# Weight loads of 448 rows over all 128 partitions, paired x loads, attention input copies on GpSimd, and a new issue order

## The chip, the core and the metric

The kernel runs on one core of a Trainium2 chip. The metric is device time in microseconds (us), from one launch to its end; the time before is the median of three runs. The core has a matrix engine (TensorE, in the profile PE for matmuls and PEld for weight loads), a vector engine (DVE), a scalar engine (ACT), GpSimd (POOL), and SyncE (SP), which here only issues DMAs. ACT issues a few DMAs too. The rows "SPq" and "ACTq" are these issues.

## What is computed

One block of a network on 2048 tokens of 448 features, in bf16: local dilated attention with 16 heads of 28 features, then a gated MLP that mixes over tokens with a 2048 by 2048 matrix.

```python
def _A_ref(x, wqkv, wo):                       # x: 1 x 2048 x 448
    qkv = (x @ wqkv).reshape(B, S, 3, 16, 28)  # q, k, v
    idx = pos[:, None] - 2 * arange(8)         # 8 keys, every second token back
    attn = softmax(q . k[idx] * 28 ** -0.5)    # masked where idx < 0
    return (attn . v[idx]).reshape(B, S, D) @ wo
def _B_ref(x, w_in, w_sp, b_sp, w_out):
    z = gelu(x @ w_in)                         # 1792 features
    z1, z2 = z[..., :896], layernorm(z[..., 896:])
    g = w_sp @ z2 + b_sp[None, :, None]        # mixes over the 2048 tokens
    return (z1 * g) @ w_out
h  = x + _A_ref(layernorm(x), wqkv, wo)
h2 = h + _B_ref(layernorm(h), w_in, w_sp, b_sp, w_out)
```

## The kernel before, in words

**Tiling.** The 2048 tokens are two halves of 1024. The normalised and transposed activations lie in `xh`, with features on partitions: the first half's tokens on partitions 0 to 63, the second half's on 64 to 127, and the 448 features as seven blocks of 64 rows along the free axis. A matmul has 64 rows, and two of them, one for each half, run side by side on the upper and the lower rows of the array. Each weight matrix therefore lies twice in SBUF: on partitions 0 to 63 and again on 64 to 127, block c on both at free index c.

**Loads.** `ld_w` (L542) loads each of Wq, Wk and Wv with two DMAs of 392 KB, the lower copy from SP and the upper copy from ACT, each to 64 partitions. Wq and Wk are staged in `z2p` and copied (L729, `cp`) into padded form in `reg1`; Wv goes straight to `reg1`. `ld_win` (L552) loads the MLP's input weights with eight DMAs of 64 partitions, `ld_x` (L536) the tokens with sixteen DMAs of 112 KB, and L920 loads Wo four times over 28 partitions each. In the profile, `z2p<-in_A_wqkv` is Wq or Wk, `reg<-in_A_wqkv` is Wv, `reg<-in_A_wo` is Wo.

**Stages.** For each unit u of 128 tokens of both halves: layer norm 1 (`bn_stats` L617, `bn_aggr` L622, the reciprocal root on ACT L633/634 or POOL L608/609, the normalisation L641 into `tring`), and the transpose into `xh`, for units 0 to 2 by PE (L657) with a copy out of PSUM, for units 3 to 7 by a transposing DMA (L648). Then the q and k matmuls (L759) and, for each of nine attention tiles i, a copy `xv` of 128 columns of `xh` (L797), v (L807), logits (L838), exp (L852), mask (L860), row sums (L873), log and exp of the reciprocal (L882, L907), the weighted sum (L896) and its scaling (L915). After that, unit by unit, Wo (L951), the residual (L960), layer norm 2, the MLP's z2 (L972) and z1 (L1015), and finally the token mixing g (L1049), its bias and gate (L1059, L1066), the output matmul (L1075), the last sum (L1083) and the store.

**Order.** The tuple SEQ holds a task order for each engine (sp, pool, dve, act, pe in this order), by task number. `replay` walks these lists and emits the instructions; engines run them strictly in that order and wait on semaphores. The numbers in `replay` (`bw`, `issue`, `costs`) choose PSUM banks and buffers and otherwise move nothing.

## Time and profile before

| | us |
|---|---|
| median of 3 runs | 258.79 (258.0 to 260.02) |
| the profiled execution: its time | 258.7 |
| the profiled execution: its span | 257.0 |
| PE busy | 233.9 (91%) |
| DVE busy | 135.6 (53%) |
| ACT busy | 89.8 (35%) |
| POOL busy | 26.0 (10%) |

A span is the time from the first to the last instruction in the trace; 1.7 us of the run's time lie outside it. Busy shares are averages over very different stages: PE is busy nearly throughout, so what counts is where it is not, and what it waits for there.

### The profile page before, as it was taken

The numbers are of one execution on the slowest core, as the hardware profiler recorded it, in microseconds if no ns is written. First come the engines' busy times: TensorE is split into PE (matmuls) and PEld (weight loads), VectorE is DVE, ScalarE is ACT, GpSimd is POOL, SyncE is SP. The second block draws the span as 40 slices with busy tenths as digits, with TensorE's granted clock in tenths as the row PEclk, the third lists the DMA queues.
The fourth block names the chain that finished last, engine by engine and source line by source line (L and its number), as shares of the span: only waits on it lengthen the run. The fifth ranks groups of instructions, "written<-read, shape, count | busy, mean of one in ns | idle before, by whom it ended". The sixth has DMA issues, their size and how long they took to land.

```text
span 257.0 us, 6304 instructions
## 1 busy us (share of the span) xinstructions
PE 233.9 (91%) x2822; PEld 123.2 (48%) x2822; DVE 135.6 (53%) x286; ACT 89.8 (35%) x107; POOL 26.0 (10%) x67
## 2 busy tenths in 40 slices
PE   0298987998688999999999999999999999999995
PEld 0276754456344585554444444444444444444542
DVE  4378946737477996977773015210063127442444
ACT  3369876599448664556574000000000000000000
POOL 7202400000100213202180000000000000000000
PEclk9999999999779999999999999999999999999999
DMA  6995089648959378898454634200000000001013
GB/s 172 207 249 106 13 121 191 77 109 146 179 70 190 70 106 210 158 151 115 95 130 77 167 81 86 44 0 0 0 3 0 0 0 3 18 0 54 26 64 126
DMA packets 57235, 23.22 MB, mean 90 GB/s; under 512 B 46696, under 2 KB 57080, under 8 KB 57208
## 3 DMA queue, kind: packets, MB, share of 16 engines
q1 hardware_dynamic: 55528, 21.38, 44.1%
q10 hardware_dynamic: 1680, 1.43, 2.4%
q8 instruction: 22, 0.36, 0.6%
q14 instruction: 5, 0.04, 0.1%
HBM read 9.60 MB, written 1.84 MB: 44 GB/s over the span
## 4 chain that ended last, share of the span: by engine, by line
PE 75%; DVE 9%; DMA 7%; ACT 4%; issue 2%; SPq 2%; POOL 1%
PE psum L1049 38%; PE psum L1075 8%; PE psum L1015 6%; PE psum L951 5%; PE psum L972 5%; DMA x_tm<-in_A_x_dram 5%; PE psum L759 5%; PE psum L807 3%; DVE tring L641 2%; DVE st L617 2%; DMA xh<-tring 2%; PE psum L896 2%; PE psum L838 1%; DVE st L988 1%; DVE xv L605 1%
## 5 line engine op out<-in xcount | busy, mean ns | idle before, releaser
L1059 DVE TENSOR_TENSOR reg<-psum,reg 128x512 bf16<-128x512 f32 x28 | 18.8, 688 | 70.8 <-PE psum L1049 60.1
L1049 PE MATMUL psum<-reg,z2p 128*128 128x512 bf16 x224 | 50.1, 379 | 0.0
L1049 PE MATMUL psum<-wspT_lo,z2p 128*128 128x512 bf16 x224 | 49.5, 379 | 0.0
L1049 PEld LDWEIGHTS psum<-wspT_lo,z2p 128*128 128x128 bf16 x224 | 21.8, 98 | 26.6 <-DVE z2p L1002 0.4
L1049 PEld LDWEIGHTS psum<-reg,z2p 128*128 128x128 bf16 x224 | 21.9, 98 | 26.1
L759 PE MATMUL psum<-xh,reg 64*128 64x256 bf16 (+2 forms) x336 | 27.3, 317 | 1.8 <-ACT reg L603 1.6
L603 ACT ACTIVATE reg<-psum 128x1024 bf16<-128x1024 f32 (+2 forms) x24 | 21.3, 920 | 10.5 <-PE psum L807 5.3
L972 PE MATMUL psum<-w_in,xh 64*128 64x448 bf16 x224 | 22.5, 349 | 0.3 <-DMA xh<-tring 0.3
L1075 PE MATMUL psum<-reg 128*128 128x448 bf16 x112 | 22.2, 352 | 0.0
L1015 PE MATMUL psum<-xh,w_in 64*128 64x512 bf16 x196 | 21.7, 376 | 0.0
L759 PEld LDWEIGHTS psum<-xh,reg 64*128 64x128 bf16 x336 | 16.6, 98 | 10.4 <-ACT reg L907 2.0
L617 DVE BATCH_NORM_STATS2 st<-x_tm 128x6 f32<-128x448 bf16 x32 | 18.8, 614 | 4.6 <-DMA x_tm<-in_A_x_dram 4.6
L988 DVE BATCH_NORM_STATS2 st<-z2p 128x6 f32<-128x448 bf16 x32 | 17.6, 610 | 3.8 <-ACT z2p L982 3.8
L807 PE MATMUL psum<-reg,xv 64*128 64x448 bf16 x126 | 15.1, 378 | 4.0 <-ACT reg L852 2.7
L982 ACT ACTIVATE z2p<-psum 128x896 bf16<-128x896 f32 x16 | 14.1, 918 | 9.8 <-PE psum L972 9.8
L852 ACT ACTIVATE reg<-psum 128x928 bf16<-128x928 f32 x18 | 16.3, 950 | 2.7 <-PE psum L838 2.6
L972 PEld LDWEIGHTS psum<-w_in,xh 64*128 64x128 bf16 x224 | 12.8, 94 | 9.1 <-DMA xh<-tring 1.1
L1025 ACT ACTIVATE reg<-psum 128x1024 bf16<-128x1024 f32 x14 | 13.7, 1026 | 8.1 <-PE psum L1015 8.1
L1075 PEld LDWEIGHTS psum<-reg 128*128 128x128 bf16 x112 | 11.0, 98 | 10.6
L915 DVE TENSOR_TENSOR reg<-psum,reg 128x912 bf16<-128x912 f32 x9 | 10.8, 1225 | 9.6 <-ACT reg L907 8.2
L1015 PEld LDWEIGHTS psum<-xh,w_in 64*128 64x128 bf16 x196 | 10.3, 94 | 10.7 <-issue 0.2
L951 PE MATMUL psum<-reg 64*128 64x448 bf16 x128 | 15.0, 377 | 0.2 <-ACT reg L603 0.2
(63 smaller groups left out, 183.8 us busy)
## 6 DMA issues: line engine op xcount, KB each, us to landing
w_in<-in_B_w_in_dram SPq DMA_DIRECT2D x4, 448.0 KB, 6.3
out_dram<-tring SPq DMA_DIRECT2D x16, 112.0 KB, 1.7
x_tm<-in_A_x_dram SPq DMA_DIRECT2D x14, 112.0 KB, 9.9
w_in<-in_B_w_in_dram SPq DMA_DIRECT2D x4, 336.0 KB, 4.9
z2p<-in_A_wqkv_dram ACTq DMA_DIRECT2D x2, 392.0 KB, 6.8
z2p<-in_A_wqkv_dram SPq DMA_DIRECT2D x2, 392.0 KB, 9.6
reg<-in_A_wo_dram SPq DMA_DIRECT2D x4, 196.0 KB
reg<-in_B_w_out_dram SPq DMA_DIRECT2D x1, 784.0 KB, 4.8
```

The source lines that it names most:

```text
L603: iss("act", lambda e: e.activation(dst, src, AF.Copy), reads=rd, writes=wr)
L617: iss("dve", lambda e: e.bn_stats(st[:, b, :], x_tm[:, b, :]), reads=[r_x[b]], writes=[rl[b]])
L759: iss("pe", lambda e, c=c, s=s, gi=gi, lhs=lhs: e.matmul(psum[:, bk[s] * 512 + cw * gi:bk[s] * 512 + cw * gi + cw], lhs, xh[64 * s:64 * s ...
L807: iss("pe", lambda e, c=c, s=s: e.matmul(psum[:, bk[s] * 512:bk[s] * 512 + D], xv[64 * s:64 * s + 64, xs[0], c, :], wv[64 * s:64 * s + 64, ...
L852: iss("act", lambda e: e.activation(E[:, es[0], 2 * n:2 * n + 2, :], pair_view(lb, 8 * JW), AF.Exp, scale=SCALE), reads=[r_bank[lb[0]], r_ ...
L951: iss("pe", lambda e, s=s, x=x: e.matmul(psum[:, bk[s] * 512:bk[s] * 512 + D], oT[64 * s:64 * s + 64, x, 128 * u:128 * u + 128], wo2[64 * ...
L972: iss("pe", lambda e, c=c, s=s: e.matmul(psum[:, zb[s] * 512:zb[s] * 512 + D], xh[64 * s:64 * s + 64, c, HX + 128 * u:HX + 128 * u + 128], ...
L988: iss("dve", lambda e, b=b: e.bn_stats(st3[:, b, k, :], z2p[:, b, D * k:D * k + D]), reads=[r_z2[b][k]], writes=[r_st3[b][k]])
L1015: iss("pe", lambda e, c=c, s=s: e.matmul(psum[:, bk[s] * 512:bk[s] * 512 + 512], w_in[64 * s:64 * s + 64, c, 128 * f:128 * f + 128], xh[64 ...
L1049: iss("pe", lambda e, b=b: e.matmul(psum[:, gb[0] * 512:gb[0] * 512 + 512], z2p[:, b, 128 * f:128 * f + 128], src[:, b, 512 * (tc % 2):512 ...
L1059: iss("dve", lambda e: e.tensor_tensor(ub[:, us_[0], :], psum[:, gb[0] * 512:gb[0] * 512 + 512], bb[:, 512 * tc:512 * tc + 512], ALU.add), ...
L1075: iss("pe", lambda e, f=f: e.matmul(psum[:, wb[0] * 512:wb[0] * 512 + D], z1p[f][:, 128 * m:128 * m + 128], w_out[:, f, :], start=(f == 0) ...
```

## The change

Each 448-row weight is now loaded by `ld_rows`: rows 0 to 383 as three blocks of 128 rows over all 128 partitions, rows 64 to 447 in the same way, and two pieces of 64 rows for the seventh index. The bytes are the same (896 rows). The row blocks then stand in another order on the upper than on the lower partitions; `ROWS` holds that order, and the matmuls take the block of `xh` that it names. This holds for Wq, Wk, Wv (four DMAs each, two from SP and two from ACT) and for both halves of w_in (four each from SP). Tokens come in four single blocks and six pairs. Wo is loaded once (two DMAs), and a copy of 64 x 3584 makes the second one (`cpwo`, which the new lists put on POOL). The `xv` copies may also go to POOL, and the new lists put all nine there. All five lists of SEQ are new.

```diff
-XV_ON = ("dve", "act")
+XV_ON = ("dve", "act", "pool")
+ROWS = ((0, 2, 4, 1, 3, 5, 6), (1, 3, 5, 2, 4, 6, 0))
 SEQ = (
-    (0, 4, 6, 19, 2, 13, 12, 7, 17, 21, 14, 20, 11, 16, 22, 9, 277, 18, 69, 15, 97, 76, 83, 90, 284, 276, 288, 279, 289,
+    (8, 0, 6, 2, 4, 11, 9, 18, 17, 22, 19, 15, 20, 13, 21, 69, 83, 280, 97, 76, 90, 287, 277, 288, 279, 285, 276, 289,
...
-        def ld_x(b, eng="sp"):
-            t_x[b] = dma(eng, "x%d" % b, lambda e: e.dma_start(x_tm[:, b, :], X[128 * b:128 * b + 128, :]),
-                         128 * D * 2, writes=[r_x[b]])
+        def ld_x(bs, eng="sp"):
+            b0, n = bs[0], len(bs)
+            t = dma(eng, "x%d" % b0, lambda e: e.dma_start(
+                x_tm[:, b0:b0 + n, :], X[128 * b0:128 * (b0 + n), :].rearrange("(b p) n -> p b n", p=128)),
+                128 * D * 2 * n, writes=[r_x[b] for b in bs])
...
+        def ld_rows(name, dst, src, res, engs, issue):
+            w = src.shape[1] * 2
+            parts = ((dst[:, 0:3, :], src[0:384, :].rearrange("(k p) n -> p k n", p=128), 384, 0),
+                     (dst[:, 3:6, :], src[64:448, :].rearrange("(k p) n -> p k n", p=128), 384, 1),
+                     (dst[0:64, 6, :], src[384:448, :], 64, 2),
+                     (dst[64:128, 6, :], src[0:64, :], 64, 3))
+            return [dma(engs[n % len(engs)], "%s%d" % (name, n), lambda e, d=d, f=f: e.dma_start(d, f), rows * w,
+                        writes=[res[k]], issue=issue if rows > 64 else 0.42) for n, (d, f, rows, k) in enumerate(parts)]
...
-            t_w[p] = [dma(eng, "w%s%d" % (p, s), lambda e, s=s: e.dma_start(
-                w_ld[p][64 * s:64 * s + 64], A_wqkv[:, c0:c0 + D].rearrange("(c p) n -> p c n", p=64)),
-                D * D * 2, writes=[r_ld[p][s]], issue=0.65, bw=350.0) for s, eng in ((0, "sp"), (1, "act"))]
+            t_w[p] = ld_rows("w" + p, w_ld[p], A_wqkv[:, c0:c0 + D], r_ld[p], ("sp", "act"), 0.6)
...
+            t_win[z] = ld_rows("win%d_" % z, w_in[:, :, FH * z:FH * z + FH], B_w_in[:, FH * z:FH * z + FH], r_win[z], ("sp",), 0.6)
...
-                                        xh[64 * s:64 * s + 64, c, off + t0:off + t0 + cw],
+                                        xh[64 * s:64 * s + 64, ROWS[s][k], off + t0:off + t0 + cw],
...
-        for n in range(4):
-            s, e_ = n // 2, n % 2
-            t_wo.append(dma("sp", "wo%d" % n, lambda e, s=s, e_=e_: e.dma_start(
-                wo2[64 * s + 32 * e_:64 * s + 32 * e_ + DH, :, :],
-                A_wo.rearrange("(g h d) n -> h d g n", g=8, h=2)[e_]), DH * 8 * D * 2,
-                writes=[r_wo[n]], deps=[c_wo0], bw=100.0))
+        for e_ in range(2):
+            t_wo.append(dma("sp", "wo%d" % e_, lambda e, e_=e_: e.dma_start(
+                wo2[32 * e_:32 * e_ + DH, :, :], A_wo.rearrange("(g h d) n -> h d g n", g=8, h=2)[e_]), DH * 8 * D * 2,
+                writes=[r_wo[e_]], deps=[c_wo0], bw=160.0))
+        tk = []
+        tk.append(add("cpwo", "pool", 3.6, lambda: copy(tk[0].eng, wo2[64:128], wo2[0:64], r_wo[0:2], [r_wo[2]]), deps=t_wo,
+                      alts={"pool": 3.6, "dve": 1.10, "act": 3.15}))
```

Where the new lists move work, at three places. First SP at the start of the program. Before (`x_tm` is the tokens, 16x448 a halo of the first half's last tokens):

```order
L537 DMA x_tm<-in_A_x_dram 128x448 x2
L567 DMA z2p<-in_A_x_dram 16x448
L537 DMA x_tm<-in_A_x_dram 128x448
L544 DMA z2p<-in_A_wqkv_dram 64x7x448
L537 DMA x_tm<-in_A_x_dram 128x448 x2
L544 DMA z2p<-in_A_wqkv_dram 64x7x448
L537 DMA x_tm<-in_A_x_dram 128x448 x7
L544 DMA reg<-in_A_wqkv_dram 64x7x448
L922 DMA reg<-in_A_wo_dram 28x8x448
L537 DMA x_tm<-in_A_x_dram 128x448
```

SP at the same place after the change:

```order
L572 DMA z2p<-in_A_x_dram 16x448
L539 DMA x_tm<-in_A_x_dram 128x448
L551 DMA z2p<-in_A_wqkv_dram 64x448
L539 DMA x_tm<-in_A_x_dram 128x448
L551 DMA z2p<-in_A_wqkv_dram 128x3x448
L551 DMA z2p<-in_A_wqkv_dram 64x448
L551 DMA z2p<-in_A_wqkv_dram 128x3x448
L539 DMA x_tm<-in_A_x_dram 128x2x448 x4
L551 DMA reg<-in_A_wqkv_dram 64x448
L539 DMA x_tm<-in_A_x_dram 128x2x448
L551 DMA reg<-in_A_wqkv_dram 128x3x448
L539 DMA x_tm<-in_A_x_dram 128x2x448
```

SP's share of Wq and Wk now stands directly behind the two token blocks that the first unit pair needs, with no other token block between them, and a Wo load is gone from this place. ACT issues its own two token blocks and then the other pieces of Wq and Wk.

Second, DVE between the last loads of tokens and the first row sums. Before:

```order
L605 COPY xh<-psum 128x7x128
L617 BN_STATS st<-x_tm 128x6
L622 BN_AGGR mv<-st 128x2 x2
L617 BN_STATS st<-x_tm 128x6
L622 BN_AGGR mv<-st 128x2 x4
L641 TENSOR_SCALAR tring<-x_tm,mv,rs 128x2x7x32 x2
L605 COPY xv<-xh 128x896
L641 TENSOR_SCALAR tring<-x_tm,mv,rs 128x2x7x32
L605 COPY xv<-xh 128x896
L641 TENSOR_SCALAR tring<-x_tm,mv,rs 128x2x7x32
L860 TENSOR_TENSOR reg<-reg,mband 128x928 x2
L641 TENSOR_SCALAR tring<-x_tm,mv,rs 128x2x7x32 x4
```

DVE at the same place after the change:

```order
L610 COPY xh<-psum 128x7x128
L622 BN_STATS st<-x_tm 128x6
L646 TENSOR_SCALAR tring<-x_tm,mv,rs 128x2x7x32 x2
L622 BN_STATS st<-x_tm 128x6 x3
L627 BN_AGGR mv<-st 128x2 x2
L865 TENSOR_TENSOR reg<-reg,mband 128x928
L627 BN_AGGR mv<-st 128x2 x2
L646 TENSOR_SCALAR tring<-x_tm,mv,rs 128x2x7x32
L865 TENSOR_TENSOR reg<-reg,mband 128x928
L627 BN_AGGR mv<-st 128x2 x2
L646 TENSOR_SCALAR tring<-x_tm,mv,rs 128x2x7x32 x3
```

The `xv` copies are gone from DVE, and the first masks (L865, before L860) stand earlier among the normalisations.

Third, POOL after the change, from the first `xv` copy to the first layer norm 2. Before, POOL has only the rs pairs, the mask's and the ones' set-up in this place:

```order
L610 COPY xv<-xh 128x896
L613 TENSOR_SCALAR rs<-mv 128x2
L614 TENSOR_TENSOR rs<-rs,nhalf 128x2
L610 COPY xv<-xh 128x896
L597 MEMSET reg 64x1792
L610 COPY xv<-xh 128x896
...
L710 MEMSET ones 128x32
...
L610 COPY xv<-xh 128x896 x2
L610 COPY reg<-reg 64x3584
L610 COPY xv<-xh 128x896
L613 TENSOR_SCALAR rs<-mv 128x2
```

The row `COPY reg<-reg 64x3584` is `cpwo`. The Wo matmul (L951 before, L958 after) reads its result. On PE that matmul stood behind 96 logit matmuls, and now its first unit stands ahead of them; before:

```order
L759 MATMUL psum<-xh,reg 128x512 x28
L807 MATMUL psum<-reg,xv 128x448 x14
L838 MATMUL psum<-reg 64x58 x96
L951 MATMUL psum<-reg 128x448 x32
L896 MATMUL psum<-reg 32x58 x32
```

PE at the same place after the change:

```order
L878 MATMUL psum<-reg,ones 32x464 x8
L901 MATMUL psum<-reg 32x58 x32
L764 MATMUL psum<-xh,reg 128x512 x28
L958 MATMUL psum<-reg 128x448 x16
L843 MATMUL psum<-reg 64x58 x96
```

The v matmuls that stood between the last q and k matmuls and these logits now come earlier.

## Rows read from the trace of the kernel before

**Rows 1.** Stages: busy (instructions) by PE, PEld, DVE, ACT, POOL; clock, DMA, GB/s

```profile
0.00:10.00 10.00, 1.67 (x14) 1.41 (x14) 4.36 (x14) 3.10 (x6) 6.00 (x22) 1.00 0.85 188
20.00:30.00 10.00, 9.27 (x245) 6.59 (x241) 8.78 (x27) 9.36 (x16) 4.45 (x13) 1.00 0.27 57
...
10.00:12.00 2.00, 0.00 (x0) 0.00 (x0) 0.24 (x1) 0.25 (x1) 0.00 (x0) 1.00 1.15 198
16.00:18.00 2.00, 2.00 (x40) 1.75 (x38) 2.00 (x4) 0.57 (x2) 0.00 (x0) 1.00 1.13 282
112.00:254.00 142.00, 141.68 (x792) 65.64 (x786) 55.83 (x124) 17.30 (x19) 7.93 (x16) 1.00 0.25 52
```

**Rows 2.** The chain that ended last, its end: start, length, what

```profile
136.14 76.08 PE psum L1049 x352
...
254.17 0.62 DVE tring L1083
```

**Rows 3.** Timeline of the start: start, length, instruction, idle before it

```profile
11.76 0.62 DVE L605 COPY reg<-z2p 128x1568 bf16<-128x1568 bf16 x1 [4.09 <-DMA z2p<-in_A_wqkv_dram]
12.30 0.48 DVE L682 TENSOR_SCALAR z2p<-z2p,mvh,rsh 16x448 bf16<-16x448 bf16 x1
12.71 0.60 DVE L605 COPY xh<-psum 128x896 bf16<-128x896 bf16 x1
13.36 7.55 PE L759 MATMUL psum<-xh,reg 64*128 64x256 bf16 x112 [0.18 <-DVE xh L605]
21.07 1.50 PE L807 MATMUL psum<-reg,xv 64*128 64x448 bf16 x14 [0.15 <-DMA reg<-in_A_wqkv_dram]
23.51 1.54 PE L838 MATMUL psum<-reg 28*64 28x58 bf16 x128
```

**Rows 4.** The chain between 27 and 40 us

```profile
27.99 0.99 DVE xv L605
...
35.08 0.44 PE psum L873 x8
```

**Rows 5.** Timeline of PE: stalls between 34 and 90 us, and the first Wo matmul

```profile
35.08 0.39 PE L873 MATMUL psum<-reg,ones 64*32 64x464 bf16 x8 [0.51 <-DVE reg L605]
39.86 3.20 PE L759 MATMUL psum<-xh,reg 64*128 64x512 bf16 x28 [1.55 <-ACT reg L603]
58.77 3.20 PE L951 MATMUL psum<-reg 64*128 64x448 bf16 x32 [0.17 <-ACT reg L603]
66.29 1.96 PE L807 MATMUL psum<-reg,xv 64*128 64x448 bf16 x14 [2.68 <-ACT reg L852]
73.53 0.21 PE L896 MATMUL psum<-reg 64*32 64x58 bf16 x6 [1.28 <-issue]
83.69 2.63 PE L807 MATMUL psum<-reg,xv 64*128 64x448 bf16 x25 [1.17 <-issue]
```

**Rows 6.** Instructions on tile xv: ns least/median/most, first and last start

```profile
L605 DVE COPY xv<-xh x7: 1069/1079/1085, 16.4 to 79.9; 128x896 bf16<-128x896 bf16 x7
L603 ACT ACTIVATE xv<-xh x2: 960/972/984, 13.3 to 61.0; 128x896 bf16<-128x896 bf16 x2
```

**Rows 7.** Timeline of POOL: its longest instruction

```profile
2.10 1.59 POOL L592 MEMSET reg<- 128x1792 f32 x1
```

**Rows 8.** Stages of 2 us after the stall at 66 us

```profile
66.00:68.00 2.00, 1.71 (x14) 0.92 (x15) 1.05 (x3) 0.07 (x1) 0.78 (x2) 0.80 1.12 241
68.00:70.00 2.00, 2.00 (x14) 1.03 (x12) 0.00 (x0) 0.92 (x1) 0.15 (x1) 0.50 1.08 207
70.00:72.00 2.00, 2.00 (x99) 1.08 (x95) 0.97 (x1) 0.62 (x1) 0.00 (x0) 0.85 0.92 150
```

**Rows 9.** Timeline of SP: the second token-mix transpose and the fourth Wo load

```profile
46.20 1.17 SPq L932 DMA_TRANSPOSE wspT_lo<-in_B_w_sp_dram  x1
47.41 0.56 SPq L922 DMA_DIRECT2D reg<-in_A_wo_dram  x1
```

**Rows 10.** Tile reg (Wv, Wo and later loads): DMA issue to landing

```profile
DMA to landing us min/median/max: 4.0/5.3/11.4
```

86 lines of the change are left out of this document (41 added, 45 removed), and 57 rows, old and new, of the table SEQ.

## The prediction

> **What bounds the kernel now.** I read the stages first, then the chain that ended last, then the timelines of the two places that they point to.
>
> From 112 us to 254 us PE is busy 141.68 us of 142 [rows 1], and the chain of that stretch is matmuls alone, up to the last sum on DVE at 254.17 and the last store [rows 2]. The change keeps every matmul there, so that half stays as long as it is, and so does the tail behind it. What can move is when PE gets there: its idle time and slow stretches before 90 us.
>
> There are three kinds. *The start.* In the first 10 us PE is busy 1.67 us [rows 1]. Its first q and k matmul runs at 13.36, directly behind three DVE instructions: the copy of Wq (11.76, which had waited 4.09 us for the load), the halo's normalisation (12.30) and the copy of unit 1 into `xh` (12.71) [rows 3]. Those three run without a gap, so Wq's landing sets PE's start. *The middle.* Between 20 and 30 us PE is busy 9.27, ACT 9.36 and DVE 8.78 us of 10 [rows 1], all three near their limit; the chain there runs through DVE, with `xv` copies on it, to the row sums at 35.08 [rows 4]. PE waits 0.51 us for DVE at 35.08, 1.55 at 39.86 and 2.68 at 66.29 for ACT [rows 5]. *Stalls in which the engine waited for nothing that the profile shows*: 1.28 us at 73.53 and 1.17 at 83.69 [rows 5]. After the stall at 66.29 the granted clock is 0.80, 0.50 and 0.85 in three stages of 2 us, which is the level of 1.2 instead of 2.4 GHz for part of them [rows 8]; the loss is 2 x (0.20 + 0.50 + 0.15) = 1.7 us.
>
> **The change, part by part.**
>
> *Weights over 128 partitions, and their place in the queue.* Wq and Wk lie behind 14 KB of halo and four token blocks of 112 KB on both queues together: 14 + 448 + 2 x 784 = 2030 KB, or 2.08 MB, and nothing else. The first 10 us moved 188 GB/s on average, issue and first latency included [rows 1]; at that pace 2.08 MB are there at 11.05 us. That is the bound without any faster transfer. Between 10 and 12 us, when the old 64-partition weight loads filled the queue, the rate was 198 GB/s; between 16 and 18, with token blocks over 128 partitions among them, 282 [rows 1]. If all 1.6 MB of Wq and Wk went at 282 in place of 198, they would take 1.6 x (1/198 - 1/282) x 1000 = 2.4 us less, so 8.6 us at best. I take 10.2, nearer to the slow end, because both weights now finish together, with Wq's last piece behind Wk's large one on ACT. The halo's normalisation now stands ahead of the copy on DVE, so PE starts at 10.2 + 0.62 + 0.60 and about 0.1 of gaps = 11.5, against 13.36: **1.9 us earlier**, with bounds of 1.0 and 3.4.
>
> The Trainium skill ("SBUF — State Buffer", Door 1: The DMA port swizzle) says that a transfer to one half of the partitions reaches only half of the DMA ports, and that only one transfer over all 128 reaches all of them. The stage rows lean its way, 198 against 282 GB/s, though they mix kinds of transfers; if it holds fully the start is at its 3.4 us bound.
>
> This gain must survive Wv, which PE met at 21.07 with a wait of 0.15 us [rows 3]. Its last pieces stand behind all but two token blocks, and ACT issues its share only after its copies of Wq and Wk. The same faster rate over 2.35 MB of weights gives Wv up to 3.5 us; I need 1.9. If the rate stays, PE waits there and the gain is 0.5 us, because PE now does unit 2's transposes while it waits.
>
> *More, smaller DMAs.* There are six more issues of weights and six fewer of tokens. ACT issues three more, at about 0.6 us each; they lie between its Wq and Wk copies, and the k matmuls follow 56 q matmuls that hide them. Nothing is added.
>
> *w_in.* Eight loads before and after, needed only at about 90 us; hidden behind the whole attention, and the mixing of row blocks costs the matmuls nothing, since their shapes are the same.
>
> *xv copies to POOL.* DVE loses seven copies of 1.08 us and ACT two of 0.97 [rows 6]. The DVE ones between 16 and 42 us lie on or next to the chain. POOL has no such copy in this trace. Its longest instruction writes 1792 elements per partition in 1.59 us, or 0.89 ns per element [rows 7], so 896 elements take 0.8 us if reading is free and 1.6 us if reading costs as much as writing. I take 1.1, nearest the same work on DVE and ACT. Queued behind them on POOL are the rs pairs of later units, which can slip by one copy, and behind these the normalisations; that hands back a part of what DVE gains.
>
> What this is worth is bounded by PE's waits: 0.51 + 1.55 us at 35 and 40 us, and 2.68 us at 66 [rows 5], so 0 to 4.74. The first two hang on masks and row sums that come about three copies late on DVE, so I take both, 2.06. The third is ACT's own queue of exps and logarithms, which loses one copy and one eviction; I take 0.3. **2.4 us earlier.**
>
> *Wo once, and a copy.* This adds a link. The second load of Wo now stands behind the second token-mix transpose and two w_in loads, where before the fourth load followed that transpose (46.20, 47.41) [rows 9]: about 48.6 with 1.2 us more of issues, less what SP gains from the two terms above, so near 45. Landing takes 5.3 us in the median of such loads [rows 10], then POOL copies 3584 elements: 3.2 us by its rate of writing, 6.4 at twice that. The end is 53.5 to 56.7, or later if `xv` copies stand ahead. PE wants Wo at 58.77 now [rows 5], and then 4.3 us earlier and 1.0 us more because 96 logit matmuls have moved behind it: 53.4. So PE waits 0.1 to 3.3 us; a part of that only replaces the wait at 66.29. **0.6 us later.**
>
> Sum: -1.9 - 2.4 + 0.6 = -3.7 us. The profiled execution took 258.7 us, 1.7 of them outside its span of 257.0; it lies at the median, so the forecast is 253.3 of span and **255.0 us** of time.
>
> **The rivals.**
>
> *The Wo copy decides (slower).* If POOL copies at 6.4 us or more and two `xv` copies of 1.6 us stand ahead, Wo is ready at 60. PE then waits 6.6 us at its first Wo matmul, and the clock drops after it as it did after the stall at 66.29, another 1.7: -4.3 + 6.6 + 1.7 = +4.0, so 262.8. For: everything on PE queues behind that matmul. Against: POOL is busy only 10% of the span before, so little stands ahead of the copy. It decides from a copy that ends after about 57.7, where the gain is gone; beyond 58.6 with the clock's drop the kernel is slower by over 1%.
>
> *POOL holds up DVE (no change).* Nine `xv` copies and a Wo copy four times as long are 13 copies; at 0.8 us that is 10.4 us. If DVE stood still for all of it, it would lose 10.4 and gain 7.6, so the middle's 2.4 us are gone and about 1 more: -1.9 + 0.6 + 1.0 = -0.3, or 258.4. For: DVE is busy 8.78 us of 10 in that stage [rows 1], so the two must overlap. Against: no row of this trace has either engine held up by the other. The Trainium skill (same page, Who interferes with whom) speaks for it: GpSimd and some DVE instructions share a pair of ports, and the later one blocks fully. By that the case would be likelier; this trace cannot tell.
>
> *The gain is spent in ACT's queue (no change).* Both waits that I count most end on ACT. If PE merely comes earlier to the same ACT queue, only the start counts: 258.7 - 1.9 + 0.6 = 257.4.
>
> *More falls away.* The two stalls without a visible cause (2.45 us) and the drop of the clock (1.7 us) may not come again in another order: 255.0 - 4.1 = 250.9. For: they follow heavy transfers, 241 and 207 GB/s at 66 to 70 us [rows 8]. Against: others can come in their place.
>
> **How the numbers follow.** A measurement of this kernel tells a difference of about 1% (2.6 us) from none. The forecast, 251.5 to 256.2, has 0.46; more falls away, 0.15; the two cases without change together 0.25; slower by the Wo copy or by a stall like it 0.14. The likeliest is the forecast. The range leaves out the far part of the last case (0.1) and little below the best (0.1): 250.0 to 260.5. Faster by over 1%: 0.46 + 0.15 = 0.61; within 1%: 0.25; slower: 0.14.
>
> **What would show it.** In the new profile the first q and k matmul stands near 11.5; the Wq copy on DVE starts near 10.2, and the rate between 4 and 10 us is above 220 GB/s. DVE has no `xv` row, and POOL's are near 1.1 us. PE has no wait over 1 us between 30 and 45 us. The first Wo matmul stands near 54 with a wait under 2 us. From 110 us to the end PE's length is the same to half a microsecond. I am wrong if Wq still lands after 11.5, if PE waits on POOL before its first Wo matmul by more than 3 us, or if a new stall before 90 us brings a second drop of the clock.

## The result and the profile after

| | before | after |
|---|---|---|
| median of the runs, us | 258.79 [258.0 to 260.02] | 252.05 [249.79 to 254.25], four runs |
| ratio to the kernel before, same chip | | 0.964, 95% interval 0.952 to 0.975 |
| the profiled execution: time, us | 258.7 | 250.46 |
| the profiled execution: span, us | 257.0 | 248.7 |
| PE busy, us | 233.9 | 231.4 |
| POOL busy, us | 26.0 | 40.7 |

The kernel became faster, and by more than the forecast of 3.7 us: by 6.7 us between the two medians, by 9.4 after the ratio, and by 5.6 in a second set of runs on another chip (median 252.95, ratio 0.978, 0.974 to 0.983). The ratio of 0.964 compares the two fast runs among the four, 249.8 and 250.5 us and not 253.6 and 254.3, with a median of 259.4 us of four runs of the kernel before. What parts its two groups of times is not shown; the experiments have two candidates.

The first view is one of three stretches of each kernel: up to the first q and k matmul, from there to the first Wo matmul, and from there to the first matmul of the token mix (136.08 us before, 127.75 after). Columns as in [rows 1].

```profile
0.00:13.36 13.36, 2.03 (x21) 1.68 (x22) 5.96 (x18) 4.63 (x8) 6.00 (x22) 1.00 0.92 190
13.36:58.77 45.41, 41.93 (x1053) 26.76 (x1054) 29.98 (x59) 34.91 (x45) 4.45 (x13) 1.00 0.67 125
58.77:136.08 77.31, 71.86 (x1189) 40.05 (x1189) 60.84 (x135) 48.52 (x55) 15.58 (x32) 0.96 0.76 132
```

The same three stretches of the changed kernel:

```profile
0.00:10.57 10.57, 1.96 (x21) 1.67 (x21) 6.36 (x17) 4.43 (x7) 4.89 (x22) 1.00 0.85 251
10.57:56.45 45.88, 41.77 (x957) 26.34 (x959) 31.46 (x56) 32.34 (x42) 15.55 (x21) 1.00 0.74 156
56.45:127.75 71.30, 69.66 (x1286) 38.56 (x1282) 58.56 (x131) 48.44 (x53) 19.49 (x33) 1.00 0.62 115
```

Length less PE's busy time is PE's idle time: 11.33, 3.48 and 5.45 us before, 8.61, 4.11 and 1.64 after. So idle time changed by -2.72, +0.63 and -3.81 us. PE's busy time changed by -0.07, -0.16 and -2.20, although the last stretch holds 97 matmuls more: the mean granted clock there was 0.96 and is 1.00. Together that is -8.33 us, the whole distance between 136.08 and 127.75. **The middle, from which the prediction drew most, gave nothing. The last stretch before the token mix, from which it drew 0.3, gave 6.0.**

The timeline of the start answers to [rows 3]:

```profile
9.37 0.63 DVE L610 COPY reg<-z2p 128x1568 bf16<-128x1568 bf16 x1 [0.96 <-DMA z2p<-in_A_wqkv_dram]
10.57 9.13 PE L764 MATMUL psum<-xh,reg 64*128 64x256 bf16 x112 [1.18 <-DVE xh L610]
21.56 1.00 PE L843 MATMUL psum<-reg 28*64 28x58 bf16 x96
```

Two stages of the loads, the last number being GB/s:

```profile
6.00:8.00 2.00, 0.56 (x6) 0.57 (x7) 1.97 (x8) 0.50 (x2) 0.89 (x2) 1.00 1.09 353
10.00:12.00 2.00, 1.43 (x14) 1.01 (x16) 1.94 (x5) 2.00 (x2) 0.00 (x0) 1.00 1.10 374
```

Wq is there 2.4 us earlier. Between 6 and 14 us the four stages moved 330 to 374 GB/s, before the change 198 to 225. PE's first q and k matmul stands 2.79 us earlier, but the 112 matmuls then take 9.13 us in place of 7.55. In both kernels they run at 10 to 16 per us up to about 16 us and at 18 to 24 per us behind that, and the earlier start puts 68 of them into the slow part in place of 40. The granted clock reads 1.00 all the way, so the cause of the slow pace stays open. At the first logit matmul 1.95 us of the gain are left.

PE's later waits answer to [rows 5]:

```profile
30.54 0.84 PE L878 MATMUL psum<-reg,ones 64*32 64x464 bf16 x16
36.55 4.00 PE L764 MATMUL psum<-xh,reg 64*128 64x512 bf16 x42 [1.82 <-ACT reg L912]
51.27 0.39 PE L878 MATMUL psum<-reg,ones 64*32 64x464 bf16 x8 [1.82 <-DVE reg L865]
56.45 1.68 PE L958 MATMUL psum<-reg 64*128 64x448 bf16 x16
71.93 0.55 PE L901 MATMUL psum<-reg 64*32 64x58 bf16 x49 [0.32 <-issue]
75.66 0.35 PE L958 MATMUL psum<-reg 64*128 64x448 bf16 x1 [0.63 <-issue]
```

The wait for DVE at the row sums (0.51) is gone, that at the 512-wide matmuls (1.55) is still there with 1.82, and a new one for a mask has come at 51.27. The first Wo matmul waits for nothing. The stalls of 2.68, 1.28 and 1.17 us are gone from their places; two of 0.32 and 0.63 without a releaser stand at 71.93 and 75.66.

The row at 36.55, like that at 39.86 in [rows 5], names ACT, and this is a misreading by the view. ACT's instruction ends only as PE starts: at 36.55 after the change, and before it at 39.87, 0.01 us behind PE's start. What ends the wait is a transposing load of `xh`. These are its issue and the time to its landing, before and after:

```profile
L648 SPq DMA_TRANSPOSE xh<-tring x1: 1309/1309/1309, 35.6 to 35.6; - x1
DMA to landing us min/median/max: 4.1/4.1/4.1
```

```profile
L653 SPq DMA_TRANSPOSE xh<-tring x1: 1227/1227/1227, 31.6 to 31.6; - x1
DMA to landing us min/median/max: 4.7/4.7/4.7
```

The loads landed at 39.61 and 36.30, and PE went on 0.25 us later each time. It does so in all 20 profiles of this case, and in 13 of them the row names the load. The load was issued 4.0 us earlier after the change and took 0.7 us longer; PE stood at that place 3.6 us earlier, so the wait stayed.

The end of the chain is PE and one last sum on DVE, as in [rows 2]:

```profile
227.27 18.55 PE psum L1082 x98
...
245.84 0.62 DVE tring L1090
```

### The profile page after: what moved, and what is told of

It is laid out like the page before. It is cut to its first block, busy times and chain, and to the rows that moved or that the text cites. A ratio compares the mean times of both kernels' runs of the same rounds, so it can differ in the third digit from the quotient of the medians.

```text
span 248.7 us, 6335 instructions
## 1 busy us (share of the span) xinstructions
PE 231.4 (93%) x2822; PEld 121.3 (49%) x2822; DVE 136.4 (55%) x280; ACT 88.1 (35%) x104; POOL 40.7 (16%) x77
## 4 chain that ended last, share of the span: by engine, by line
PE 79%; DVE 11%; ACT 3%; DMA 2%; POOL 2%; ACTq 1%; issue 1%; DVEq 0%; POOLq 0%
PE psum L1056 39%; PE psum L979 9%; PE psum L1082 9%; PE psum L1022 9%; PE psum L764 7%; PE psum L958 4%; DVE reg L865 3%; DMA z2p<-in_A_wqkv_dram 2%; ACT reg L608 2%; DVE tring L646 2%; PE psum L812 2%; DVE st L622 2%; DVE x_tm L967 1%; DVE reg L610 1%; POOL rs L614 1%; PE psum L901 1%
## 5 line engine op out<-in xcount | busy, mean ns | idle before, releaser
L1056 PE MATMUL psum<-reg,z2p 128*128 128x512 bf16 x224 | 49.0, 379 | 0.0
L1056 PE MATMUL psum<-wspT_lo,z2p 128*128 128x512 bf16 x224 | 48.8, 379 | 0.0
L764 PE MATMUL psum<-xh,reg 64*128 64x256 bf16 (+2 forms) x336 | 28.9, 330 | 3.0 <-ACT reg L912 1.8
L608 ACT ACTIVATE reg<-psum 128x1024 bf16<-128x1024 f32 (+2 forms) x23 | 20.5, 917 | 9.9 <-PE psum L764 8.5
L764 PEld LDWEIGHTS psum<-xh,reg 64*128 64x128 bf16 x336 | 17.3, 103 | 12.4 <-ACT reg L608 2.2
L1022 PE MATMUL psum<-xh,w_in 64*128 64x512 bf16 x196 | 22.2, 376 | 0.0
L614 POOL TENSOR_TENSOR rs<-rs,nhalf 128x2 f32<-128x2 f32 x19 | 16.1, 846 | 1.6
L1022 PEld LDWEIGHTS psum<-xh,w_in 64*128 64x128 bf16 x196 | 11.0, 94 | 9.9 <-ACT reg L1032 0.5
L646 DVE TENSOR_SCALAR tring<-x_tm,mv,rs 128x448 bf16<-128x448 bf16 x32 | 14.6, 486 | 2.0 <-POOL rs L614 1.7
L865 DVE TENSOR_TENSOR reg<-reg,mband 128x928 bf16<-128x928 bf16 x18 | 13.5, 775 | 3.8 <-ACT reg L857 3.8
```

The lines of the kernel that those rows point to most:

```text
L608: iss("act", lambda e: e.activation(dst, src, AF.Copy), reads=rd, writes=wr)
L614: iss("pool", lambda e: e.tensor_tensor(dst, dst, nh, ALU.pow), reads=rr + [r_nhalf], writes=rr)
L646: iss("dve", lambda e: e.tensor_scalar(tring[:, h[0], :].rearrange("p (c s q f) -> p s q c f", c=NC7, s=2, q=2)[:, n], x_tm[:, b, :].rearr ...
L764: iss("pe", lambda e, k=k, s=s, gi=gi, lhs=lhs: e.matmul(psum[:, bk[s] * 512 + cw * gi:bk[s] * 512 + cw * gi + cw], lhs, xh[64 * s:64 * s ...
L865: iss(tk[0].eng, lambda e: e.tensor_tensor(ev, ev, mk, ALU.mult), reads=[r_E[es[0]][n], r_mband], writes=[r_E[es[0]][n]])
L1022: iss("pe", lambda e, c=c, s=s: e.matmul(psum[:, bk[s] * 512:bk[s] * 512 + 512], w_in[64 * s:64 * s + 64, c, 128 * f:128 * f + 128], xh[64 ...
```

## The experiments

Ratios are to the kernel before on the same chip, with 95% intervals; the medians of the kernel before were 258.2 to 259.4 us in the six sets.

| run | what it is | median us | ratio |
|---|---|---|---|
| e2 | before, layout of all weights | 253.08 | 0.980 (0.975 to 0.984) |
| e5 | before, layout of Wq, Wk, Wv only | 256.65 | 0.993 (0.988 to 0.997) |
| e6 | before, layout of w_in only | 258.6 | 0.995 (0.989 to 1.001) |
| e3 | before, xv copies on POOL | 257.74 | 1.000 (0.997 to 1.003) |
| e15 | before, layout and xv on POOL | 252.84 | 0.979 (0.974 to 0.984) |
| e11, e14 | new lists, 64-partition loads, xv and Wo's copy off POOL | 257.65, 255.65 | 0.998, 0.991 (0.988 to 0.994) |
| e1 | after, 64-partition loads | 255.14 | 0.986 (0.981 to 0.992) |
| e7, e13 | after, xv on DVE and ACT | 256.75, 253.52 | 0.991, 0.982 (0.976 to 0.987) |
| e8 | after, Wo copied in four pieces | 252.48 | 0.972 (0.959 to 0.986) |
| e4 | after, Wo copied on DVE | 249.96 | 0.968 (0.964 to 0.972) |
| e12 | after, once more | 252.95 | 0.978 (0.974 to 0.983) |
| e9 | after, ACT's order of loads | 250.66 | 0.971 (0.966 to 0.976) |
| e10 | e9 and e4 together | 249.06 | 0.963 (0.958 to 0.969) |
| e17 | e15, two moves on PE | 251.09 | 0.973 (0.968 to 0.977) |
| e16 | before, two moves on PE | 258.01 | 0.998 (0.995 to 1.002) |
| e18 | before, one move on SP | 265.79 | 1.023 (1.017 to 1.028) |

### The layout of the loads

One run takes the layout out of the change, three put all or parts of it alone into the kernel before.

```diff
-  (dst[:, 0:3, :], src[0:384, :].rearrange("(k p) n -> p k n", p=128), 384, 0),
+  (dst[0:64, 0:6, :], src[0:384, :].rearrange("(k p) n -> p k n", p=64), 384, 0),
```

> The changed kernel with its lists, queues and number of DMAs as they are, but each weight piece goes to 64 partitions (six blocks of 64 rows each to the lower and to the upper half) and the row order is plain again. If the layout sets the rate (341 GB/s between 8 and 14 us after, 198 before), the rate falls to about 200, the first q and k matmul moves from 10.57 to about 13, and the time rises by 2 to 3 us. If the place in the queue did it, the first matmul moves by less than 0.7 us and the time by less than 1.

> The kernel before with its lists, where each weight load is replaced by the three-block load over all 128 partitions and its piece of 64 rows; nothing else changes. If the layout sets the rate, the copy of Wq starts near 9.5 in place of 11.76, and PE near 11.3 in place of 13.36. Of that the old lists keep 1 to 2 us if PE's later waits hang on the start, and nothing if they hang on the queues of DVE and ACT. The drops of the clock at 67 and 74 us should still be there, since the lists are.

In e1 the first q and k matmul stands at 13.76 us, as late as before (e11 and e14, which have the same loads, 13.25 and 14.18), and in e2 at 11.38 us. The stage from 6 to 8 us moved 228 GB/s in e1 and 331 in e2, which stands below it with its third stretch:

```profile
6.00:8.00 2.00, 0.00 (x0) 0.00 (x0) 0.79 (x3) 0.39 (x2) 0.67 (x2) 1.00 1.07 228
```

```profile
6.00:8.00 2.00, 0.67 (x7) 0.68 (x8) 1.54 (x6) 0.50 (x3) 1.43 (x4) 1.00 1.09 331
...
56.79:130.48 73.69, 68.77 (x1188) 35.67 (x1190) 60.92 (x136) 48.72 (x55) 15.58 (x32) 1.00 0.78 137
```

The start is the layout's, and it is worth the 2 us that the prediction gave it. But the layout alone, in the old lists, gave 5 us. The last row (e2's third stretch) shows where the profile has the rest: PE is busy 68.77 us there, 3.1 less than before with the same work, because the granted clock stays at 1.00; its idle time, 4.92, is nearly that of before. Two runs should tell which weights do it:

> The kernel before, with its own lists, and only Wq, Wk and Wv in two loads over all 128 partitions and the row blocks of their matmuls to match; w_in stays in four loads of 64 partitions. The kernel before with all weights over 128 partitions took 253.1 us (before 258.2) and its profile had none of the two drops of the clock. Theory A (the later loads do it: w_in over 128 partitions is off the queues sooner, and so the stalls of PE and the drops between 63 and 78 us fall away): here the start gains 2 us, the first q and k matmul stands at 11.4, but the two drops stay, 1.7 us each: 255.5 to 256.5 us. Theory B (the earlier start does it: the heavy stretch falls elsewhere against the loads): the drops are gone here too, 252.5 to 254 us. Theory C (the drops come by chance of an execution and belong to neither): drops here or not, with single times that lie 1.5 us and more apart.

> The kernel before, with its own lists, and only w_in over all 128 partitions (two large and two small loads for each half, the row blocks of its matmuls to match); Wq, Wk and Wv stay as they were. The start is then that of before, first q and k matmul at 13.4. Theory A (w_in off the queues sooner removes the drops of the clock): 254 to 255.5 us, granted clock 1.00 up to 110 us. Theory B (the earlier start removes them): 257.5 to 258.5 us, with one or two stretches of about 3.4 us at half the clock between 63 and 78 us, as before.

Neither does it alone. Wq, Wk and Wv by themselves gave 0.993 with one drop of the clock in the profile and w_in by itself 0.995, not told from nothing. The mean clock that each run lists says more: it lay between 0.986 and 1.000 in e2's four runs and between 0.980 and 1.000 in those of the kernel before, so drops come and go between executions of one kernel (theory C), and a single profile's drops are no property of it. The two parts together gave 0.020 and their sum is 0.012; that difference is within what the three intervals allow.

### The xv copies on POOL

```diff
-XV_ON = ("dve", "act")
+XV_ON = ("dve", "act", "pool")
```

> The kernel before with all nine xv copies moved to POOL, in places that answer to their old ones; all else as before. If DVE's and ACT's load made the waits at 35, 40 and 66 us (0.51, 1.55 and 2.68), they shrink, the drop of the clock after 66 us goes with the last, and the time falls by 2 to 4 us. If POOL holds DVE up by as much as it takes off it, masks and normalisations take longer by the 0.94 us of a copy here and there and the time stays within 1 us.

In the lists the nine xv tasks moved to POOL. The ratio is 1.000. PE still waits 1.75 us at 40.23, for the transposing load, and its stalls at 65, 73 and 84 us are still there. That the copies are worth something only beside the layout or in the new lists was tested from both sides:

> The kernel before, in its own lists, with all weights over 128 partitions and the nine xv copies on POOL; Wo is loaded four times, as before. The layout alone gave a ratio of 0.980, the copies alone 1.000; the changed kernel with Wo's copy on DVE, which differs from this one by its lists, 0.968. If layout and copies carry the change and the lists only hold them: 0.966 to 0.972. If the copies are worth something only where the lists have moved other work into the room that they leave: 0.978 to 0.982, and PE's waits and stalls between 60 and 85 us stay as with the layout alone.

> The changed kernel with seven of the nine xv copies back on DVE and two on ACT, at about the places where they stood before; Wo's copy stays on POOL. Theory 1 (the change of engine is worth what the prediction gave the middle): the row sums that stand at 30.5 us in the changed kernel wait for masks again, by up to three copies of 1.08 us, the time is 251.5 to 252.5 us against about 250. Theory 2 (what DVE gains it loses again while POOL holds it, and the layout of the loads carries nearly all): 249.5 to 250.5 us, no mask longer than 0.7 us but those beside Wo's copy.

e15 has the ratio of the layout alone. e7 seemed to say otherwise, over 3 us slower than the changed kernel, but it had a fault: I had put the last two copies so late on DVE that PE waited for them, and the kernel's planner filled that wait with eight matmuls on a constant (1.90 us at 79.28).

So it was made again with the copies early and without filler:

> The changed kernel with seven xv copies on DVE and two on ACT, the last two now right behind the instruction that frees their buffers (about 66 and 68 us), and no filler matmuls. Up to 73 us its forerunner ran as the changed kernel did, so the copies before that cost nothing there. Theory 1 (DVE is full between 60 and 80 us, 9.4 and 9.9 us of 10, so each copy put there delays the masks and sums behind it, and PE): waits of PE for DVE between 68 and 82 us that add up to 1.5 to 2.2 us more than in the changed kernel, ratio to before 0.983 to 0.988. Theory 2 (the changed kernel's own slack takes them, and the loss before was only their late place): ratio 0.975 to 0.98, as the changed kernel.

Its ratio is 0.982, that of the changed kernel 0.978 (e12). It does have waits of theory 1, 0.75 and 1.01 us for DVE at 69 and 73 us (a third of 0.84 at 78 us, put down to DVE as well, ends 1.56 us behind a packet of code, which is a stall of the kind described below); one of them:

```profile
72.74 0.39 PE L854 MATMUL psum<-reg,ones 64*32 64x464 bf16 x8 [1.01 <-DVE reg L841]
```

but not the wait beside Wo's copy that the changed kernel has. The difference of the two ratios, 0.8 us, lies well inside their intervals. Against the changed kernel's first set (0.964, 0.952 to 0.975) it is 4.6 us, though. So the copies are worth nothing that these runs can tell in the old lists, with or without the layout; in the new lists the runs leave it open.

### The lists

The new lists, with e1's loads, the xv copies in DVE's and ACT's lists and Wo's copy on DVE:

> The new lists with each edit beside them undone: weights in 64-partition pieces, the xv copies on DVE and ACT, Wo's copy (loaded twice) on DVE. If the lists alone are worth nothing, and the layout (2.7 us when Wq, Wk and Wv alone have it, 5.1 with w_in) and the xv copies on POOL carry the change: 257.5 to 260 us. If the order itself carries two or more us: 253 to 256 us.

> The new lists with the other edits undone, as before, but with the last two xv copies early on DVE and no filler matmuls. If the lists are worth nothing by themselves: ratio 0.99 to 1.0. If the late copies alone hid their worth: about 0.98.

e11 had e7's fault. e14 gave 0.991, 2.3 us. On top of layout and copies the lists, with the paired token loads and the single load of Wo, are the step from e15 to e4, 0.979 to 0.968, some 3 us. PE's idle time between its first Wo matmul and the token mix shows them best: 4.6 to 5.9 us in all six profiles with the old order on PE (before, e2, e3, e5, e6, e15), 1.0 to 2.7 in the six with the new lists, 128-partition loads and xv on POOL (3.2 in e13, with xv on DVE and ACT).

### What the stalls without a cause are

In the old lists PE stops at the same places, whatever the other edits are. One lies inside the 64 averaging matmuls of a tile, all of whose operands are there: in five of the six profiles with PE's and SP's old lists. (The sixth, e6, stands 4.49 us at the place before it, at 68.14, and not here.) The timelines of PE of the kernel before, of e3, e2 (its second part) and e15:

```profile
71.62 0.63 PE L896 MATMUL psum<-reg 64*32 64x58 bf16 x58
```

```profile
73.39 0.25 PE L871 MATMUL psum<-reg 64*32 64x58 bf16 x8 [1.85 <-issue]
```

```profile
70.19 0.22 PE L911 MATMUL psum<-reg 64*32 64x58 bf16 x7 [2.63 <-issue]
```

```profile
69.37 0.22 PE L886 MATMUL psum<-reg 64*32 64x58 bf16 x9 [1.59 <-issue]
```

6, 8, 7 and 9 of 64 are left each time (the 6 in [rows 5]). What is missing is not data but code. The places are counts of instructions. Before its stalls at 66.29, 73.53 and 83.69 the kernel before has run 1242, 1370 and 1625 matmuls and about as many weight loads. The run e16, described below, has other matmuls at the first two places of its list and stops behind the same three counts. The first two for each (PE and PEld are the first and the second count):

```profile
0.00:66.28 66.28, 48.80 (x1242) 31.67 (x1243) 42.49 (x86) 46.23 (x59) 10.46 (x35) 1.00 0.73 139
0.00:73.52 73.52, 54.76 (x1370) 34.86 (x1370) 44.66 (x90) 49.25 (x63) 11.38 (x37) 0.98 0.74 140
```

```profile
0.00:66.54 66.54, 51.14 (x1242) 32.98 (x1243) 41.42 (x85) 44.58 (x58) 10.46 (x35) 1.00 0.74 137
0.00:74.67 74.67, 55.65 (x1370) 35.31 (x1370) 44.80 (x90) 49.70 (x63) 11.39 (x37) 0.99 0.75 139
```

The table of DMA queues has two for instructions, with 22 and 5 packets in an execution. The trace does not name their engines. But 0.36 MB in 22 packets, over PE's 5644 matmuls and weight loads, are 64 bytes each and 256 instructions to a packet, which is the distance between the first two stalls; DVE, the next, has 286 instructions. So I take this queue for PE's. In all 20 profiles a stall of half a microsecond or more without a releaser ends 1.2 to 1.6 us behind the end of one of its packets (64.72, 72.11 and 82.16 in the kernel before).

This holds for the stall at 66.29 too (1.58 us), which [rows 5] puts down to an exp on ACT. That exp ended 0.23 us before PE went on, where a result of DVE lets PE go on after 0.06. In e18 (below), with the same count and 1.45 us behind its packet, PE goes on at 66.955, and the exp that the view names ends at 66.963. In e2, e3, e5 and e15 PE stops two to four instructions before that count, among the logits, and no releaser is named. So all three stalls are late code.

In the kernel before the queue has no packet between 68 and 71 us, while the 16 engines are full (113.3% of them), and one between 71 and 73 (71.03 to 72.11), at the end of the traffic; PE goes on at 73.53:

```profile
q1 hardware_dynamic: 816, 0.58, 113.3%
...
q1 hardware_dynamic: 508, 0.12, 29.4%
q8 instruction: 1, 0.02, 3.4%
```

In the changed kernel, between 68 and 72 us, the packet is the only traffic, and PE still stops for 0.32 us:

```profile
DMA packets 1, 0.02 MB, mean 4 GB/s; under 512 B 0, under 2 KB 0, under 8 KB 0
q8 instruction: 1, 0.02, 1.4%
```

What fills them stands in SP's list. In the kernel before SP issues two transposing loads of `w_sp` from 66.77 on; in the changed one it stands, until 71.76, at a transposition that waits for DVE:

```profile
66.77 7.94 SPq L932 DMA_TRANSPOSE wspT_lo<-in_B_w_sp_dram  x2
```

```profile
60.69 2.15 SPq L939 DMA_TRANSPOSE wspT_lo<-in_B_w_sp_dram  x1
71.76 1.25 SPq L653 DMA_TRANSPOSE xh<-tring  x1
```

The Trainium skill ("Runtime: NRT & Kernel Launch", Instruction fetch mechanics) says that each engine's code streams in by its own DMA queue in blocks of 16 KiB, and that the cost is mostly hidden. The size agrees (22 packets, 0.36 MB). "Mostly hidden" doesn't, here: single blocks cost PE up to 4.49 us (e6).

Three runs bear on the two sides of this, how fast PE uses its code up and what stands ahead of it in the DMA engines. Full DMA engines ahead of the packet are not needed for a stall: in e2 they were 11 to 15% busy from 58 to 61 us, the packet started at 60.57, and PE stopped for 1.54 us before 63.18. The move on PE:

```diff
-    ..., 225, 228, 205, 234, 202, 342, 210, 235, 212, 213, 232, 264, ...
+    ..., 225, 228, 202, 205, 234, 342, 210, 235, 232, 212, 213, 264, ...
```

(202 and 232 are groups of 14 v matmuls, 205, 234 and 235 logit matmuls, 212 and 213 the averaging ones.)

> The old lists with the layout and the xv copies on POOL, and two moves on PE alone: 14 v matmuls (1.5 us) from behind the 64 logit matmuls to ahead of them, and the next 14 from behind the 64 averaging matmuls to ahead of them, so that small matmuls stand less close together. Without the moves it took 252.84 us, ratio 0.979, with stalls of 1.96 us at 63.38 and 1.59 at 69.37. Theory 1 (PE runs out of loaded code where small matmuls follow each other closely; the order of its list sets that): the two stalls together fall from 3.55 to under 1.5 us, about 251 us. Theory 2 (PE stops after a fixed count of instructions however they are mixed, or because of the other engines): the stalls stay at 3 to 4 us in sum, at other matmuls, 252.5 to 253 us. Rival beside both: the v matmuls come before their bank or their xv copy is there and wait for ACT or POOL instead.

> The kernel before with the same two moves on PE and nothing else. Its stalls at 66.29 (2.68 us, put down to ACT) and 73.53 (1.28, put down to nothing) stand at the same places of the list as the two stalls without cause in the other kernels with the old lists. Theory 1 (code that is not loaded in time, by the density of small matmuls): the two together fall from 3.96 to under 2 us, 256.5 to 257.5 us. Theory 2 (ACT's exps really hold the first): the first stays at 2 us and more, now in front of the logit matmuls or of the transposed sums, 258 to 259 us.

With the new layout (e17) the stalls fell from 3.55 to 0.59 us, of which a part came back as waits of 0.80 us for ACT and 0.79 for DVE; the median is 1.75 us lower than e15's. In the kernel before (e16) the first fell to 0.91, but the second grew, and the time stayed: 

```profile
74.69 0.34 PE L871 MATMUL psum<-reg 64*32 64x58 bf16 x20 [3.62 <-issue]
```

There the code came from 72.33 us on, again behind the loads: between 68 and 72.3 us the DMA engines are full (114.5%) and hold no packet of code. So the last run left PE alone and made SP stand still, by moving one transposition (312) ahead of two loads of w_in and two of w_sp:

```diff
-    ..., 292, 287, 293, 280, 281, 294, 295, 282, 312, 296, ...
+    ..., 292, 287, 293, 312, 280, 281, 294, 295, 282, 296, ...
```

> The kernel before with one move on SP alone: the transposing DMA of unit 0 of the second layer norm, which waits for DVE until about 75 us, now stands ahead of two loads of w_in (now issued at 63.31) and two transposing loads of w_sp (66.77), so that SP stands still and the DMA engines are idle from about 66 to 75 us, as in the changed kernel. Theory 1 (PE's code lands late behind these loads): the stalls at 66.29 (2.68 us) and 73.53 (1.28) shrink to under 2 us in sum, those that are left belong to ACT, and w_in is still there at 90 us: 256 to 257 us. Theory 2 (the loads have no part in it): both stalls stay within half a microsecond, 258.5 to 259.5 us. Rival beside both: w_in comes too late for the second token mix at 90 us and gives the gain back there.

The kernel is 2.3% slower, by the rival named there: w_in now comes too late, and PE waits for it at 93 us.

```profile
66.95 2.80 PE L782 MATMUL psum<-reg,xv 64*128 64x448 bf16 x14 [2.44 <-ACT reg L827]
73.46 0.68 PE L871 MATMUL psum<-reg 64*32 64x58 bf16 x64
...
93.31 0.53 PE L947 MATMUL psum<-w_in,xh 64*128 64x448 bf16 x1 [4.69 <-DMA w_in<-in_B_w_in_dram]
```

But in its profile (of one of its six executions) the second stall is gone: the 64 averaging matmuls run in one piece. So is the one at 83.69. The first stays with 2.44 us; its packet had started at 64.18, before the quiet stretch. ACT's row for the exp named there:

```profile
66.02 0.94 ACT L827 ACTIVATE reg<-psum 128x928 bf16<-128x928 f32 x1
```

The packet behind the first stall starts 2.58 us after its end in e18 (69.53), without other traffic, and 4.74 us after it in the kernel before (71.03), with the DMA engines 112% busy. So the loads do hold the code of the second stall up. They are not the only reason that it is gone: at a lower granted clock for longer, PE also reached that place later. For the stall at 83.69 the loads are argued, not shown. The changed kernel is rid of all but 0.95 us of its code stalls without e18's price: all its w_in loads are issued by 73.1 us, before the change the last one at 89.2. How much of this its order on PE did and how much the quieter queue is not parted.

### Wo's copy on POOL

The copy holds DVE. These are three views of the changed kernel: POOL's timeline, the chain that ended last with the two masks on DVE beside the copy, and all masks by tile (ns least, median, most).

```profile
45.32 3.17 POOL L610 COPY reg<-reg 64x3584 bf16<-64x3584 bf16 x1 [9.52 <-DMA reg<-in_A_wo_dram]
```

```profile
45.60 3.94 DVE reg L865 x2
```

```profile
L865 DVE TENSOR_TENSOR reg<-reg,mband x18: 576/626/3387, 24.5 to 78.3; 128x928 bf16<-128x928 bf16 x18
```

One mask took 3.39 us in place of 0.63, and PE's wait at 51.27 is for the masks behind it. The Trainium skill ("SBUF — State Buffer", Who interferes with whom) says so of a DVE instruction with two inputs in SBUF, as a mask is, beside a GpSimd instruction that reads; the trace agrees.

```diff
-    ..., 216, 201, 278, 231, ...          # POOL: 278 is Wo's copy
+    ..., 216, 201, 231, ...
-    ..., 179, 192, 136, ...               # DVE
+    ..., 179, 192, 278, 136, ...
```

> The changed kernel with the second copy of Wo made on DVE, behind the two masks of 45.6 us, in place of POOL. If POOL's copy of 3.17 us holds the mask that takes 3.39 us in place of 0.63, every mask takes under 0.7 us here, PE's wait of 1.82 us before the row sums at 51.27 goes, and the time falls by 1.5 to 2 us. If that wait has another end behind it (ACT or PSUM), the mask is short again but the time stays within 0.5 us.

> The changed kernel with the copy of Wo on POOL in four instructions of 64 x 896 elements, each about 0.8 us, in place of one of 64 x 3584 (3.17 us). In the changed kernel a mask on DVE that began at 45.60, beside that copy, took 3.39 us where the median is 0.63, and PE then waited 1.82 us at 51.27 for it. Theory 1 (POOL holds what DVE shares for the length of one instruction, and DVE gets its turn between two): no mask longer than about 1.5 us, PE's wait shrinks to under 1 us, about 249.3 us. Theory 2 (DVE stands as long as POOL has copies): one mask of over 2.5 us or several of over 1.2 us beside the copies, the same wait, 250 us. Moving the copy to DVE gave 249.96 with that wait gone.

On DVE the copy takes 1.09 us, no mask is over 0.64, and the four times lie between 249.8 and 250.3, though the profiled execution began its q and k matmuls only at 13.02. In four pieces on POOL the longest mask took 1.36 us, and in place of the wait of 1.82 us PE has one for DVE of 0.35. The masks by tile, and POOL's timeline:

```profile
L865 DVE TENSOR_TENSOR reg<-reg,mband x18: 577/629/1360, 27.1 to 79.3; 128x928 bf16<-128x928 bf16 x18
```

```profile
49.25 4.87 POOL L610 COPY reg<-reg 64x896 bf16<-64x896 bf16 x4 [10.87 <-DMA reg<-in_A_wo_dram]
```

So DVE gets its turn between two instructions of POOL (the four pieces took 4.87 us in place of 3.17). Its time is not better than the changed kernel's; its start was the latest of the profiles with this layout, 13.37 us.

The wait may have a second price. The changed kernel run once more:

> The changed kernel itself, once more, beside the three. If the start's scatter is real, its profile has the copy of Wq on DVE anywhere from 9.4 to 12.2 us and its times again lie from 249.8 to 254.3 us; the median 250.5 to 253.5.

Its timeline of PE at that place, and two stages behind it:

```profile
51.95 0.39 PE L878 MATMUL psum<-reg,ones 64*32 64x464 bf16 x8 [1.95 <-DVE reg L865]
```

```profile
54.00:56.00 2.00, 2.00 (x18) 0.78 (x18) 1.23 (x1) 1.97 (x3) 0.00 (x0) 0.50 1.29 249
56.00:58.00 2.00, 2.00 (x16) 0.74 (x12) 1.23 (x1) 0.89 (x2) 0.00 (x0) 0.65 0.35 69
```

After the wait the granted clock falls to 0.50, its level of 1.2 GHz, and PE, busy throughout, loses 2 x (0.50 + 0.35) = 1.7 us. In e7 and e9 such a drop follows a wait of 2.04 us at the same place; e4 and e8, with 0.28 and 0.35 us there, have none. Every one of e12's four runs lists a mean clock of 0.992 or 0.993, which is one such drop; e4's four list 0.999 to 1.000. Of the changed kernel's four runs the profiled one, 250.46 us, had no drop, after a wait of 1.82 us; 254.25 and 253.64 list 0.993, but so does 249.79. So a drop does not part the two groups of its times by itself, and the start of the three others is not on record.

### The start's scatter, and a faster kernel

In six profiles with the changed kernel's order of loads Wq's copy began at 9.37 to 12.16 us. The last piece of Wq stands behind Wk's large piece in ACT's queue.

```diff
-    (1, 3, 12, 5, 10, 7, 37, 50, ...      # ACT: x8, x9, wk3, wq1, wk1, wq3
+    (1, 3, 7, 5, 12, 10, 37, 50, ...      # ACT: x8, x9, wq3, wq1, wk3, wk1
```

> The changed kernel with one difference: ACT issues the two pieces of Wq that it loads (48 and 336 rows of its queue: the small one, then the large one) ahead of its two pieces of Wk, where now Wq's small piece stands behind Wk's large one. In four profiles with the changed kernel's order the copy of Wq on DVE began at 9.37, 10.77, 11.82 and 12.16 us. Theory 1 (that last small piece, behind ACT's share of Wk in a queue that SP's queue outruns, sets the start and its scatter): here the copy begins between 8.5 and 9.6 us, the first q and k matmul stands at 9.8 to 10.8, and the times lie together at 249 to 250.5 us instead of from 249.8 to 254.3. Theory 2 (the start does not reach the end, as the kernel with Wo's copy on DVE suggests, which began at 13.02 and ended as early): the start comes early, but times scatter as those of the changed kernel, median 251 to 252.5.

> The changed kernel with ACT's pieces of Wq ahead of those of Wk and with Wo's copy on DVE behind the masks, in place of POOL. Wo's copy on DVE alone gave 249.96 us with a start at 13.02. If both gains are whole: the start 2 us earlier and nothing late next, 248 us. If the 512-wide q and k matmuls, which wait for transposed tokens or for ACT at 36 to 39 us, swallow the start's gain: 249.5 to 250 us. The candidate that could beat both kernels.

(The small pieces have 64 rows, the large ones 384; the figures in the first expectation are KB and rows mixed up.) Beside e12 on one chip e9's median is 2.3 us lower, and its times lie within 1.3 us. Its profile doesn't show why: Wq's copy began at 9.89 us, e12's at 10.08, and the first q and k matmul stands at 11.29 in both. With Wo's copy on DVE as well the copy of Wq began at 8.90 and the median is 249.06: 1.5% below the changed kernel on that chip, the fastest version of the study.

## Why the prediction was right and wrong

**The start: right in the sum, by luck.** The forecast was 1.9 us for PE's first q and k matmul. That came 2.79 us earlier (10.57 for an estimated 11.5), because Wq landed 0.8 us before its estimate: the loads ran at 330 to 374 GB/s, above the 282 that I had as the upper bound. The 112 matmuls behind it then took 1.58 us longer, which the prediction does not have. That 1.95 us were left at the first logit matmul (1.57 in e12) is two misses that cancel. That the start scatters by up to 2.8 us I did not see either. The Trainium skill ("SBUF — State Buffer", Door 1: The DMA port swizzle) has the faster rate for all 128 partitions; the traces agree, 330 to 374 GB/s against 198 to 225.

**The middle: a step that failed.** I took 2.06 us for the waits at 35 and 40 us, as masks and row sums that come late on DVE. The middle's idle time rose by 0.63 us. The first wait, 0.51, went, but it went in e3 too, whose time did not change. The second was never DVE's or ACT's: it is a transposing load of `xh` that lands 4.1 to 4.7 us after its issue, and PE only came to it earlier (1.55, then 1.82 us). My rival "the gain is spent in ACT's queue" has the right outcome for this term and the wrong cause. The xv copies that the term rests on are worth nothing in the old lists: 1.000 alone, 0.979 against 0.980 with the layout. POOL's price for a copy was nearly right (1.1 forecast, 0.94 measured).

**The third wait: the step that failed most.** I read the 2.68 us at 66.29 as ACT's own queue of exps and took 0.3 of it. It was late code, as were the two stalls that the forecast put at nothing. The last stretch before the token mix, from which the forecast drew 0.3, gave 6.0: 3.81 of idle time and 2.20 of PE's busy time, where two drops of the clock are gone and 97 more matmuls have come. A releaser that the view names is a guess; its end against PE's start, 0.23 us where 0.06 to 0.15 is usual, would have raised the doubt.

**Wo's copy: wrong place, and dearer.** I took 0.6 us. Neither its wait of 0.1 to 3.3 us at the first Wo matmul nor the rival of 262.8 came. The copy took 3.17 us, as its lower bound, but it started at 45.32 and held a mask, and PE waited 1.82 us at 51.27. "POOL holds up DVE" was the rival whose mechanism is real; its time of 258.4 did not come, since it let all 13 copies hold DVE. Undoing the long one gave 1.6 us (e9 to e10).

**"More falls away": the rival that came, at 0.15.** It said 250.9; the profiled execution took 250.46. That it lies so near is partly luck: it keeps the 2.06 us of the middle, which did not come, and leaves out most of the stall at 66.29 and a second drop of the clock. I had counted 2.45 us of stalls without cause and one drop. These stalls went but for 0.95 us, and the second drop stood between 74 and 78 us, outside the stages of [rows 8] that I had read. The evidence for a cause stood in the trace: a stall in the middle of a group of equal matmuls whose operands are there is no wait for data, and the instruction queue's packets can be asked for by window. With it I would have looked at SP's list, which the change cleared of heavy loads there, and given this case more than the forecast.

**The tail: right.** From its first token mix matmul to the end PE takes 120.9 us before (136.08 to 257.0) and 121.0 after (127.75 to 248.7).
